# Where ScalarE puts the older rows' share of a token mix: the bank of the values, or an SBUF tile of its own

## The chip, the cores and the metric

The kernel runs on one NeuronCore of a Trainium2 chip. The metric is the device time of one execution in microseconds; lower is better. The engines are TensorE (PE, with its weight loads as PEld), VectorE (DVE), ScalarE (ACT), GpSimd (POOL) and SyncE (SP), which here only issues DMAs. Each engine works through its own queue in order and meets the others at semaphores.

## The reference

An attention with a soft cap is followed by a channel mix with a gate. Cut to what matters:

```python
def _attn_ref(q, k, v, cap):                    # (8, 12, 448, 64) each
    scores = cap * np.tanh(q @ k.T / sqrt(64) / cap)
    attn = np.exp(scores - scores.max(-1))
    attn = attn / (attn.sum(-1) + 1e-09)
    return attn @ v

def _moe_ref(x, mu_k, mu_r, w_k, w_v, w_r):     # x: (8, 448, 768)
    x_prev = concat([zeros, x[:, :-1]], axis=1)  # the row before
    xk = mu_k * x + (1.0 - mu_k) * x_prev
    xr = mu_r * x + (1.0 - mu_r) * x_prev
    k = np.maximum(xk @ w_k, 0.0)
    v = k * k @ w_v
    r = 1.0 / (1.0 + np.exp(-(xr @ w_r)))
    return r * v
```

The product `(1.0 - mu_k) * x_prev` in the line of `xk` is what the change is about.

## The kernel before

**Stages.** Up to about 510 us of the execution the kernel works through 48 pairs of heads (8 batches by 6 pairs; a pair fills 128 partitions, 64 channels of each of two heads, and its 448 tokens lie along the free dimension). In the same stretch it splits the weights into a high and a low part, and multiplies the mixed rows of the batch before by `w_k` (the matmuls on `kps`, K in the lists of steps). From about 510 us it finishes the last batch's product with `w_k` and then runs the products with `w_v` and `w_r` (line 702), which the change does not touch.

**A pair's way.** Scores of a pair's keys in groups of 128 (S0, S1, S2, and the last 64 keys of one or two pairs as S3) go into `s`, two PSUM tiles of two banks each. ScalarE applies tanh (line 290) and exp (line 303) into `p`. PE multiplies by the values into `pv` (V, lines 314 and 330). VectorE sums `p` with a transposing reduction (red, line 339); four small DMAs on SP gather these sums (line 345), VectorE ends them and inverts them (recip, lines 349 to 356), and they go out to DRAM (line 359) and come back spread over the partitions as `r` (line 368). Then three instructions follow each other on two engines:

```python
# norm, line 372, VectorE: reads pv (PSUM) and r, writes x
self.nc.vector.tensor_mul(self.X[i % 2][:, 1:], self.PV[i][:, 0:S], self.R.pop(i))
# mix_old, line 382, ScalarE: (1 - mu_k) * the row before, written over pv
self.nc.scalar.mul(self.xold, self.X[i % 2][:, 0:S], self.om["k"][:, hp:hp + 1])
# mix_new, line 387, VectorE: mu_k * x + xold
self.nc.vector.scalar_tensor_tensor(out=self.xk, in0=self.X[i % 2][:, 1:], scalar=self.mu["k"][:, hp:hp + 1],
                                    in1=self.xold, op0=ALU.mult, op1=ALU.add)
```

After mix_new GpSimd splits `xk` into `xkh` (line 124) and `xkl` (line 134), the operands of K. GpSimd also splits q and k of a later pair (`qkh` in line 124, `qkl` in line 134; `qkl` is a subtraction of two SBUF tiles over 896 columns) and the weights (`wkh`, `wkl`, line 584).

**What orders the work.** Each engine's queue is written out by hand as lists of step names (`STEP_0`, `STEP_6`, `STEP_7`, `ROWS`, `LAST` and others), one list per pair i; V in list i belongs to pair i-1, and norm, mix_old and mix_new to pair i-2. So in list i mix_old stands behind some tanh and exp on ScalarE, and mix_new behind some of the reductions and in front of the others, and of the weights' instructions, on VectorE.

**The bank.** `pv` has two buffers (`ps_v`, one bank each). V of pair k+2 therefore takes the bank that pair k had, and its first matmul waits for the last instruction that read or wrote that bank. In the kernel before that is mix_new of pair k, since `xold` lies in the bank. The pool `up` holds small SBUF tiles (`r`, `xk`, `xg`, `rs`), and `xk` has one buffer there.

Below, norm(k), mix_old(k) and mix_new(k) are those of pair k, and V(k) is its product with the values.

Of the kernel before, what the change touches and what calls it, by code (L numbers as in the profile page):

```python
# [10 lines left out]
F32 = mybir.dt.float32  # L11
# [6 lines left out]
B, H, S, D = 8, 12, 448, 64  # L18
# [11 lines left out]
P = 128  # L30
# [79 lines left out]
class Body:  # L110
# [263 lines left out]
    def mix_old(self, i):  # L374
        b, hp = i // NP, i % NP
        if hp == 0:
            xh = self.xkp[b % 2].tile([P, ND, S], F32R, name="xkh", tag="xkh")
            xl = self.xkp[b % 2].tile([P, ND, S], F32R, name="xkl", tag="xkl")
            self.XK[b] = (xh, xl)

        self.xold = self.PV.pop(i)[:, 0:S]
        self.nc.scalar.mul(self.xold, self.X[i % 2][:, 0:S], self.om["k"][:, hp:hp + 1])

    def mix_new(self, i):
# [682 lines left out]
```

## Time and profile before

| | |
|---|---|
| median of 3 runs | 908.24 us (905.85 to 908.97) |
| the profiled execution | 909.15 us, of which the span of the instructions is 907.3 us |
| PE busy | 873.5 us, 96% of the span |
| VectorE busy | 727.3 us, 80% |
| ScalarE busy | 624.0 us, 69% |
| GpSimd busy | 413.0 us, 46%, nearly all of it before 500 us |
| mean granted TensorE clock | 0.993 |

The profile is of one execution. "Busy" adds the instructions' durations; matmuls are pipelined, so a busy PE need not be at its peak. Idle time is put down to whatever the waiting instruction got last. A wait on an engine costs time only where the work that follows is itself on the way to the end, so the shares of this table say little on their own.

### The profile page before, as it was taken

Reading aid. Unit: us, or ns where it says so; the run is one execution under the profiler, and the core shown is the slowest. Engines: PE = TensorE matmul, PEld = TensorE weight load, DVE = VectorE, ACT = ScalarE, POOL = GpSimd, SP = SyncE. Lnnn points to the kernel's source line nnn. Section 1 sums busy time; section 2 is a strip of 40 time slices with the busy share of each in tenths; the row PEclk is TensorE's granted clock in tenths of the full one; section 3 lists DMA queues with packets and bytes.
Section 4 is the critical chain, followed back from the end, with each engine's and each line's share of the span. In section 5 each row is a group of like instructions: output and inputs, shape, how many; then the busy total and the mean of one; then the engine's idle time right before and its main releaser. Section 6 shows DMA issues by size and latency. Waiting matters only on the chain.

```text
span 907.3 us, 16778 instructions
## 1 busy us (share of the span) xinstructions
PE 873.5 (96%) x5826; PEld 703.6 (78%) x5826; DVE 727.3 (80%) x1246; ACT 624.0 (69%) x925; POOL 413.0 (46%) x345
## 2 busy tenths in 40 slices
PE   6889999999999999999999899999999999999996
PEld 2235666767767667667767699999999999999996
DVE  6888985988898998889878656787888667777775
ACT  8897887877878878788877365556565535555553
POOL 5895584777777776777763200000000024443330
PEclk9899999999999999999999999999999999999999
DMA  5465746676676767667566455745445546777663
GB/s 164 154 202 171 235 149 171 195 210 203 190 216 199 220 192 200 205 192 224 165 204 184 140 199 172 246 147 170 151 155 165 172 147 186 221 216 222 215 219 112
DMA packets 123679, 170.15 MB, mean 188 GB/s; under 512 B 22592, under 2 KB 107712, under 8 KB 123584
## 3 DMA queue, kind: packets, MB, share of 16 engines
q1 hardware_dynamic: 120992, 164.88, 59.6%
q10 hardware_dynamic: 2592, 4.10, 1.2%
q8 instruction: 48, 0.79, 0.4%
q14 instruction: 47, 0.39, 0.1%
HBM read 109.91 MB, written 56.60 MB: 184 GB/s over the span
## 4 chain that ended last, share of the span: by engine, by line
PE 58%; DVE 20%; DMA 8%; ACT 6%; SPq 4%; issue 4%; POOL 0%; DVEq 0%; ACTq 0%; POOLq 0%
PE ps L702 39%; DVE r L339 6%; PE kps L489 6%; PE pv L314 4%; DMA sq__195<-r 4%; PE kps L464 4%; SPq L345 3%; ACT p L303 3%; PE s L277 3%; ACT p L290 2%; DMA r<-rec_d 2%; DVE wsq L568 2%; DVE wa L571 2%; DMA rec_d<-rs 1%; DVE xk L387 1%
## 5 line engine op out<-in xcount | busy, mean ns | idle before, releaser
L290 ACT ACTIVATE p<-s,scl_t 128x896 f32<-128x896 f32 (+1 forms) x172 | 166.5, 980 | 37.0 <-PE s L277 20.9
L339 DVE TRANSPOSE_TENSOR_REDUCE r<-p 128x28 f32<-128x896 f32 (+1 forms) x192 | 180.1, 968 | 7.5 <-ACT p L303 7.0
L303 ACT ACTIVATE p<-p,cap_t 128x896 f32<-128x896 f32 (+1 forms) x172 | 174.4, 1023 | 4.3 <-ACT ko L501 0.4
L314 PE MATMUL pv<-p,rv 128*64 128x448 f32 x576 | 124.6, 562 | 14.3 <-DVE xk L387 14.2
L666 POOL TENSOR_TENSOR s<-src 128x384 f32<-128x384 f32 x14 | 14.3, 1020 | 266.3 <-DVE lo L687 266.3
L702 PE MATMUL ps<-wvh,hi 128*128 128x384 f32 x392 | 131.0, 334 | 0.0
L702 PE MATMUL ps<-wvl,hi 128*128 128x384 f32 x392 | 131.0, 334 | 0.0
L686 ACT CAST hi<-s 128x512 fp32r<-128x512 f32 (+1 forms) x112 | 63.6, 568 | 89.6 <-PE ps L702 76.9
L489 PE MATMUL kps<-xkh,wkh 64*128 64x448 f32 (+1 forms) x540 | 116.0, 370 | 3.3 <-ACT ko L501 3.3
L687 DVE TENSOR_TENSOR lo<-s,hi 128x512 fp32r<-128x512 f32 (+1 forms) x112 | 70.1, 626 | 59.4 <-ACT hi L686 43.8
L489 PE MATMUL kps<-xkh,wkl 64*128 64x448 f32 (+1 forms) x540 | 113.3, 362 | 0.0
L489 PE MATMUL kps<-xkl,wkh 64*128 64x448 f32 (+1 forms) x540 | 112.9, 361 | 0.0
L134 POOL TENSOR_TENSOR qkl<-rqk,qkh 128x896 fp32r<-128x896 f32 x47 | 100.4, 2136 | 10.2 <-ACT qkh L128 6.7
L702 PE MATMUL ps<-wrh,hi 128*128 128x384 f32 x294 | 98.9, 336 | 0.3 <-DVE o L725 0.3
L702 PE MATMUL ps<-wrl,hi 128*128 128x384 f32 x294 | 98.8, 336 | 0.0
L314 PEld LDWEIGHTS pv<-p,rv 128*64 128x64 f32 x576 | 36.5, 138 | 75.9 <-issue 48.6
L686 ACT CAST hi<-src 128x512 fp32r<-128x512 f32 (+1 forms) x84 | 47.8, 569 | 62.7 <-PE ps L702 59.7
L702 PE MATMUL ps<-wvh,lo 128*128 128x384 f32 x392 | 83.7, 334 | 0.0
L584 POOL TENSOR_TENSOR wsq<-wa,wsq 128x384 f32<-128x384 f32 (+1 forms) x40 | 54.3, 1357 | 54.6 <-DVE wsq L577 50.0
L489 PEld LDWEIGHTS kps<-xkh,wkh 64*128 64x128 f32 (+1 forms) x540 | 63.9, 184 | 18.0 <-ACT ko L501 6.4
L687 DVE TENSOR_TENSOR lo<-src,hi 128x512 fp32r<-128x512 f32 (+1 forms) x84 | 56.8, 677 | 21.5 <-ACT hi L686 19.3
L702 PEld LDWEIGHTS ps<-wvh,hi 128*128 128x128 f32 x392 | 73.6, 188 | 0.1
(118 smaller groups left out, 1928.0 us busy)
## 6 DMA issues: line engine op xcount, KB each, us to landing
rqk<-qk SPq DMA_DIRECT2D x47, 448.0 KB
src<-k_d SPq DMA_DIRECT2D x56, 256.0 KB
rv<-v SPq DMA_DIRECT2D x48, 256.0 KB
r<-rec_d SPq DMA_DIRECT2D x96, 112.0 KB
v_d<-o SPq DMA_DIRECT2D x56, 192.0 KB
src<-x_d SPq DMA_DIRECT2D x42, 256.0 KB
vl<-v_d SPq DMA_DIRECT2D x56, 192.0 KB
out<-o SPq DMA_DIRECT2D x55, 192.0 KB
```

Of the source, the lines that this page charges most:

```text
L134: {"p": self.nc.gpsimd, "v": self.nc.vector}[e].tensor_sub(*a)
L277: nc.tensor.matmul(s[:, (h + i) % 2, 0:S], qk[a][p, k], qk[b][p, 0:S], start=(n == 0), stop=(n == 2))
L290: self.nc.scalar.activation(p32[:, n], self.S.pop((i, g))[:, n, 0:S], AF.Tanh, scale=self.scl_t)
L303: self.nc.scalar.activation(p32, p32, AF.Exp, scale=1.0 if self.maxima else self.cap_t)
L314: nc.tensor.matmul(pv[p, 0:S], v[:, g, h, :], ph[:, (h + i) % 2, :], start=(g == 0), stop=False)
L339: self.nc.vector.tensor_reduce(out=r1[:, 0:RM].rearrange("p (x g) -> p x g", g=3)[:, :, g] if g < 3 else r1[:, RM:RC], in_=p32.rearrange(" ...
L464: nc.tensor.matmul(self.kps[fc][:, 0:S], w, m[:, dc, :], start=first, stop=last)
L489: self.nc.tensor.matmul(self.kps[c][:, 0:S], w[p, dc, c * P:(c + 1) * P], m[p, dc, :], start=s == 0, stop=last or way == 2 and t == 2, ski ...
L584: {"p": self.nc.gpsimd, "v": self.nc.vector}[e].tensor_add(sq, f(a), sq)
L686: self.nc.scalar.copy(hi, x)
L687: self.nc.vector.tensor_sub(lo, x, f(hi))
L702: self.nc.tensor.matmul(o, a[:, c, :], w[:, c, :], start=first and k == 0, stop=last and k == len(todo) - 1, skip_group_check=True)
```

## The change

ScalarE's product no longer overwrites the bank of the values. It goes into an SBUF tile `xold` of 128 by 448 floats with one buffer, from the pool `up`. The bank is no longer used after norm.

```diff
-        self.xold = self.PV.pop(i)[:, 0:S]
+        self.PV.pop(i)
+        self.xold = self.up.tile([P, S], F32, name="xold", bufs=1)
         self.nc.scalar.mul(self.xold, self.X[i % 2][:, 0:S], self.om["k"][:, hp:hp + 1])
```

So mix_old writes SBUF where it wrote PSUM; mix_new reads both of its inputs from SBUF where one came from PSUM; the first matmul of V(k+2) waits for norm(k) in place of mix_new(k); and mix_old(k+1) must wait until mix_new(k) has read the one buffer. No instruction is added, removed or reordered.

## Rows read from the trace of the kernel before

**Rows 1.** The page's head: span of all instructions.
```profile
span 907.3 us, 16778 instructions
```
**Rows 2.** Windows: stretch, busy time of each engine (instructions), granted clock, DMA share.
```profile
20.00:80.00 60.00, 49.85 (x260) 20.95 (x258) 52.89 (x89) 52.56 (x65) 51.03 (x45) 0.94 0.55 172
...
300.00:400.00 100.00, 97.70 (x810) 69.25 (x808) 89.33 (x156) 80.24 (x104) 73.94 (x58) 1.00 0.70 207
```
**Rows 3.** Waits: engine and line, releaser, total us, times, longest us.
```profile
POOL xkh L124 <- DVE xk L387: 83.5, 38, 8.6
...
PE pv L314 <- DVE xk L387: 14.2, 11, 3.4
```
**Rows 4.** Instructions by source line: count, duration in ns (min/median/max), first and last start.
```profile
L382 ACT ACTIVATE pv<-x,om_k x48: 618/639/644, 30.6 to 519.2; 128x448 f32<-128x448 f32 x48
...
L426 ACT ACTIVATE xl<-xo,om_r x14: 657/659/672, 548.0 to 713.8; 128x448 f32<-128x448 f32 x14
...
L387 DVE SCALAR_TENSOR_TENSOR xk<-x,mu_k,pv x48: 626/626/682, 32.0 to 519.9; 128x448 f32<-128x448 f32 x48
...
L399 DVE SCALAR_TENSOR_TENSOR xg<-x,mu_r,xg x34: 676/680/1341, 161.8 to 513.7; 128x448 f32<-128x448 f32 x34
```
**Rows 5.** The chain that ended last, first 560 us: start, us, what.
```profile
56.12 6.40 DMA rec_d<-rs
...
69.86 2.48 PE pv L314 x12
...
504.77 4.06 PE pv L314 x12
```
**Rows 6.** Timeline around 30 us: start, us, engine, line, tiles, [idle before <-releaser].
```profile
29.90 0.63 DVE L372 TENSOR_TENSOR x<-pv,r 128x448 f32<-128x448 f32 x1 [1.17 <-DMA r<-rec_d]
...
32.69 1.76 PE L314 MATMUL pv<-p,rv 128*64 128x448 f32 x4 [3.41 <-DVE xk L387]
```
**Rows 7.** Timeline of POOL and of DVE, 40 to 51 us.
```profile
40.33 2.12 POOL L134 TENSOR_TENSOR qkl<-rqk,qkh 128x896 fp32r<-128x896 f32 x1
...
49.55 2.10 POOL L134 TENSOR_TENSOR qkl<-rqk,qkh 128x896 fp32r<-128x896 f32 x1
...
40.92 0.64 DVE L387 SCALAR_TENSOR_TENSOR xk<-x,mu_k,pv 128x448 f32<-128x448 f32 x1
...
42.06 0.55 DVE L573 SCALAR_TENSOR_TENSOR wa<-w,kps 128x384 uint32<-128x384 uint32 x1
...
45.37 1.11 DVE L339 TRANSPOSE_TENSOR_REDUCE r<-p 128x28 f32<-128x896 f32 x1 [0.55 <-ACT p L303]
...
49.87 0.64 DVE L387 SCALAR_TENSOR_TENSOR xk<-x,mu_k,pv 128x448 f32<-128x448 f32 x1
```
**Rows 8.** Timeline of POOL, ACT and DVE, 67 to 92 us.
```profile
70.78 1.33 POOL L134 TENSOR_TENSOR xkl<-xk,xkh 128x448 fp32r<-128x448 f32 x1
...
89.54 2.13 POOL L134 TENSOR_TENSOR qkl<-rqk,qkh 128x896 fp32r<-128x896 f32 x1
...
86.43 1.16 ACT L501 ACTIVATE ko<-kps 128x448 f32<-128x448 f32 x2 [2.24 <-PE kps L464]
...
67.08 0.63 DVE L372 TENSOR_TENSOR x<-pv,r 128x448 f32<-128x448 f32 x1 [1.42 <-DMA r<-rec_d]
...
71.15 1.78 DVE L573 SCALAR_TENSOR_TENSOR wa<-w,wa 128x768 uint32<-128x768 uint32 x1
...
91.10 0.68 DVE L387 SCALAR_TENSOR_TENSOR xk<-x,mu_k,pv 128x448 f32<-128x448 f32 x1 [2.45 <-ACT pv L382]
```
**Rows 9.** Timeline around the last V, 498 to 514 us.
```profile
498.89 0.59 DVE L372 TENSOR_TENSOR x<-pv,r 128x448 f32<-128x448 f32 x1
...
503.92 1.04 ACT L303 ACTIVATE p<-p,cap_t 128x896 f32<-128x896 f32 x1
...
504.77 4.06 PE L314 MATMUL pv<-p,rv 128*64 128x448 f32 x12 [2.78 <-DVE xk L387]
...
513.67 0.54 ACT L501 ACTIVATE ko<-kps 128x448 f32<-128x448 f32 x1 [0.64 <-PE kps L464]
```

## The prediction, made before the result

> **What bounds the kernel now.** I began with the head of the page: the instructions span 907.3 us [rows 1], and the execution's own 909.15 us lies 1.85 us above that. Next the windows of the first stage, the only one that the change touches [rows 2]. From 20 to 80 us no engine is full: PE 49.85 of 60, VectorE 52.89, ScalarE 52.56, GpSimd 51.03. They hand work round in a ring. From 300 to 400 us PE has 97.70 of 100 and VectorE 89.33, so there PE is the bound and VectorE is not far behind it. The list of waits says what the bank costs: PE stood 14.2 us in 11 waits for mix_new before a V, while GpSimd stood 83.5 us in 38 waits for the same instruction and can afford it [rows 3]. Then the durations of the two instructions that change, with the nearest ones that already work in SBUF [rows 4].
>
> 14.2 us is not the gain. A wait counts only where it lies on the chain that ended last, and of the 11 only three are followed there by the V that they hold up: V(2), V(6) and V(47). V(6) and V(47) are shown [rows 5]. The other eight V are not in the chain: had they started sooner, PE would have stood later, for ScalarE or for GpSimd's weights.
>
> **What the earlier release is worth.** V(k+2) may start at the end of norm(k).
>
> V(2): norm(0) ends at 29.90 + 0.63 = 30.53, V(2) started at 32.69 after 3.41 us of standing [rows 6], so it can start 2.1 us sooner. ScalarE, fed by the scores behind V(2), would run about 1.2 us ahead at its next tanh. But VectorE is the slower one here: from 39 us on it works without a break but for 0.55 us at 45.37, where it waited for an exp [rows 7]. More than 0.55 us cannot be passed on.
>
> V(6): norm(4) ends at 67.08 + 0.63 = 67.71, V(6) started at 69.86 [rows 5, 8]: 2.1 us for PE. It is passed on, because ScalarE stands 2.24 us for PE's product at 86.43 and VectorE then 2.45 us for mix_old at 91.10 [rows 8]. 2.1 us.
>
> V(47): norm(45) ends at 499.48, PE has been free since 502.0, V(47) started at 504.77 and took 4.06 us [rows 9], where V(6) took 2.48 [rows 5]. After the change two of its three groups of keys can run from 502.0; the third needs the exp that ends at 503.92 + 1.04 = 504.96. A third of 2.48 us is 0.83, so V(47) would end at 505.8 and not at 508.83: 3.0 us. Next late is the bank of `kps` in the K that follows: its release, the relu at 513.67, came just after the product (0.64 us of standing) and stands on ScalarE behind mix_old(46), which ends at 513.03. A product that is ready 3 us sooner finds ScalarE still before mix_old(46), so the relu moves by 0.6 us only; PE, working 12 matmuls of 0.2 us on the other bank meanwhile, stands about 0.6 us. 2.4 us remain. After 510 us PE stands 0.3 us in all until about 900, so what arrives there arrives at the end.
>
> Gains: 2.1 + 2.4 = 4.5 us, and up to 0.55 at V(2).
>
> **What the SBUF tile costs.** mix_old: the like instruction that writes SBUF has a median of 659 ns, mix_old 639 [rows 4]: 20 ns by 48 is 1.0 us on ScalarE, which mostly hides behind its waits; 0.2 us on the chain. The wait for the one buffer costs nothing: mix_new(k) has ended a list earlier.
>
> mix_new alone: the nearest row with both inputs in SBUF is line 399, 680 ns against 626 [rows 4]; line 573 with one input in PSUM took 0.55 us for 384 columns [rows 7], which scaled to 448 is about mix_new's present length, so the lower end is nothing. Some 15 of the 48 mix_new lie in the chain: 0 to 0.8 us, I take 0.4.
>
> mix_new beside GpSimd is the large item. Line 573 with one input in PSUM starts at 42.06 while GpSimd is inside `qkl` (40.33 to 42.45), and takes its 0.55 us [rows 7]. With both inputs in SBUF it starts at 71.15 while GpSimd is inside `xkl` (70.78 to 72.11), and takes 1.78 us for twice the columns: it stands until GpSimd's instruction ends [rows 8]. Line 399 goes from 676 to 1341 ns at its worst [rows 4]. The mix_new of before runs beside GpSimd undisturbed, 682 ns at most; after the change it is of the second kind. The Trainium skill, "SBUF — State Buffer", section "Who interferes with whom", states this as a rule: a VectorE instruction with two SBUF inputs contends with a GpSimd instruction that reads SBUF, and the later one is held back. These rows agree.
>
> Over the timeline, 16 of 48 mix_new start inside a GpSimd instruction; what was left of it adds up to 9.1 us. In 38 GpSimd was itself waiting for `xk` [rows 3]; where both hold, `qkl` reached only 0.1 to 0.6 us into mix_new. The long ones lie early. mix_new(1) at 40.92 meets `qkl` until 42.45, 1.5 us; mix_new(2) at 49.87 meets one until 51.65, 1.8 us [rows 7]. VectorE is the slower engine there, so 1.5 less the 0.55 of slack is passed on, 0.95 us. For mix_new(2) and mix_new(3) it is a toss: GpSimd is late too, since it waits for `xk` and the weights from VectorE, and its `qkl` then starts within 0.2 us of mix_new's turn. First come, mix_new pays little; second, 1.9 us. Some of that is taken up by the trip of the reciprocals to DRAM, 6.40 us at 56.12 [rows 5], which other transfers hold up. I take 1.4 us for the three, with ends of 0 and 4.5.
>
> mix_new(6): ScalarE is 2.1 us sooner, but a GpSimd split in front of the `qkl` at 89.54 costs 0.4. Had mix_new come 0.6 us later, it would stand until that `qkl` ends at 91.67 [rows 8], and V(6)'s gain would be gone. mix_new(7), (8) and (9) meet a split of weights each, 0.3 us, 0.9 in all, in a stretch from 91 to 130 us in which VectorE never stands. mix_new(10) meets 1.66 us of `qkl`, which a wait for `r` behind it covers; uncovered, all of it would count. mix_new(11) meets 0.6 and holds up the reciprocals of the next pair: 0.5. Six later ones of 0.1 to 0.2 us: 0.3.
>
> Costs: 0.2 + 0.4 + 1.4 + 0.4 + 0.9 + 0.5 + 0.3 = 4.1 us.
>
> **Sum.** 909.15 - 4.5 + 4.1 = 908.75 us for an execution like the profiled one; the 0.55 of V(2) is already set against mix_new(1). The median of the runs is 0.91 us under that execution, so I forecast 907.8.
>
> **Rivals.** What a measurement here can tell from no change is 0.3%, 2.7 us.
>
> *The port is cheap, and the release is all.* If GpSimd's instruction only delays mix_new's start a little, or if mix_new comes first after the shift, the gains stand: 909.15 - 4.5 - 0.55 = 904.1, or 903.2 by the median; with 0.9 us for the lengths, 904.1. For it: most mix_new find GpSimd waiting. Against it: the 1.78 us of line 573.
>
> *VectorE held behind `qkl` becomes the bound of the first 70 us.* Place: mix_new(1), (2) and (3). Price: 1.5 + 1.9 + 1.9 less 0.55 is 4.75 us in place of 1.4; it decides if GpSimd's `qkl` starts first each time. That alone is 907.8 + 3.35 = 911.2, slower. For it: GpSimd works from 36 to 67 us without a break, and the two queues run in step. Against it: for mix_new(3) the order before was the other one. This is the rule of the skill just named, with each turn going against mix_new.
>
> *An input from SBUF is quicker.* If mix_new were 65 ns shorter, its share of the chain would give 15 by 65 ns = 1.0 us in place of costing 0.4, and the sum 906.4, still no change. The Trainium skill, "Perfetto Trace Analysis", section "Optimizing Scalar/DVE Operations", gives VectorE about 60 ns of access time on SBUF and 125 on PSUM, from which the 65 are estimated. Line 399, longer than mix_new [rows 4], speaks against it.
>
> *The bank is not released sooner.* If V(47) and V(6) waited for something beside mix_new, only costs would be left: 908.24 + 4.1 = 912.3. The release at the end of norm is plain in the order of the code, so it is the least likely.
>
> **How the numbers follow.** Gain and port about cancel (905.5 to 910.9, the likeliest's own range): 0.47, and the quicker input 0.02 within it. The release is all: 0.26. VectorE held behind `qkl`: 0.23. No earlier release: 0.04. So faster 0.26, same 0.47, slower 0.27. The range runs from 903.8, which keeps most of the first rival, whose full gains of 5.05 us and cheap lengths give 903.2 to 904.1, to 911.8, which takes in the second with a little of the lengths' upper end; about 1 in 10 is left on each side.
>
> **What would show it.** Right: no wait of PE for mix_new; V(47) starts by 502.1 and takes its last group at 505; V(6) starts within 0.1 us of norm(4)'s end; mix_new's median stays near 626 to 680 ns but its maximum goes to about 2 us, and the long ones are among mix_new(1) to (11), with `qkl` beside them; after V(47) PE stands for the relu for about 0.6 us. Wrong: mix_new's maximum below 0.8 us (the port term falls, and the time is near 904), or norm(4) more than 3 us later than before (the toss went against VectorE each time, and the time is over 911), or V(6)'s 2.1 us taken back before 130 us.

## The result, and the profile after

The change makes the kernel slower by half a per cent: 912.47 us median of 10 runs (909.69 to 916.73) against 907.9 us (10 runs of the kernel before), a ratio of 1.0052 with a 95% interval of 1.0033 to 1.0070. The forecast was 907.8 us, no change, with a range up to 911.8. The profiled execution took 915.32 us, 2.85 us above the median of its kernel, so its trace shows somewhat more loss than a typical execution. Lines of the changed kernel lie one higher from mix_old on: mix_old is line 383, mix_new 388, the relu 502, K 465 and 490.

The head of the page, beside [rows 1]:
```profile
span 913.5 us, 16777 instructions
```
The windows beside [rows 2]. From 20 to 80 us PE and VectorE are busy 2.4 and 1.8 us longer; from 300 to 400 us, where PE is the bound, PE is busy 0.9 us less, at a granted clock of 0.98 in place of 1.00:
```profile
20.00:80.00 60.00, 52.23 (x264) 21.28 (x260) 54.64 (x88) 52.45 (x65) 51.75 (x44) 0.94 0.53 172
300.00:400.00 100.00, 96.84 (x788) 67.90 (x784) 89.21 (x153) 78.73 (x102) 72.67 (x58) 0.98 0.69 201
```
The waits beside [rows 3]. PE's 14.2 us for mix_new are gone; 1.9 us for norm are left. PE's waits for the relu (before 3.3 us in 5, at most 0.7) are now fewer and longer:
```profile
POOL xkh L124 <- DVE xk L388: 84.7, 40, 8.6
...
PE kps L490 <- ACT ko L502: 6.1, 4, 2.7
...
PE s L277 <- ACT p L290: 5.7, 8, 2.1
...
PE pv L314 <- DVE x L372: 1.9, 2, 1.5
```
The durations beside [rows 4]. Alone, mix_new costs 10 ns more in the median with two SBUF inputs, mix_old 31 ns; only the maximum of mix_new is new:
```profile
L383 ACT ACTIVATE xold<-x,om_k x48: 652/670/674, 30.0 to 526.5; 128x448 f32<-128x448 f32 x48
...
L388 DVE SCALAR_TENSOR_TENSOR xk<-x,mu_k,xold x48: 629/636/2337, 31.5 to 527.2; 128x448 f32<-128x448 f32 x48
```
The timeline at mix_new(1), beside [rows 7]. It starts 0.25 us after `qkl` and ends 0.5 us behind the end of `qkl` at 42.24, so it stands nearly as long as `qkl` runs:
```profile
40.14 2.10 POOL L134 TENSOR_TENSOR qkl<-rqk,qkh 128x896 fp32r<-128x896 f32 x1
40.39 2.34 DVE L388 SCALAR_TENSOR_TENSOR xk<-x,mu_k,xold 128x448 f32<-128x448 f32 x1
```
The timeline at V(6), beside [rows 5, 8]. V(6) waits for nothing at 68.86, 1.4 us behind the end of norm(4) (0.1 us was predicted), but PE stood 2.14 us just before, for a tanh:
```profile
66.84 0.62 DVE L372 TENSOR_TENSOR x<-pv,r 128x448 f32<-128x448 f32 x1
...
68.05 0.47 PE L277 MATMUL s<-qkh 64*128 64x448 f32 x2 [2.14 <-ACT p L290]
68.86 1.47 PE L314 MATMUL pv<-p,rv 128*64 128x448 f32 x4
```
The timeline around 200 us, which the prediction did not look at. ScalarE stands 3.33 us for norm(16), then does mix_old and two exps, and only then the relu that PE needs; PE stands 2.68 us:
```profile
198.82 0.62 DVE L372 TENSOR_TENSOR x<-pv,r 128x448 f32<-128x448 f32 x1 [0.65 <-DMA r<-rec_d]
199.48 0.67 ACT L383 ACTIVATE xold<-x,om_k 128x448 f32<-128x448 f32 x1 [3.33 <-DVE x L372]
200.05 1.96 ACT L303 ACTIVATE p<-p,cap_t 128x896 f32<-128x896 f32 x2
201.92 0.95 ACT L502 ACTIVATE ko<-kps 128x448 f32<-128x448 f32 x2
...
202.49 1.17 PE L490 MATMUL kps<-xkh,wkh 64*128 64x448 f32 x2 [2.68 <-ACT ko L502]
```
The windows there: behind this stand TensorE is granted the lower of its two levels (1.2 GHz) for a while; (1 - 0.73) and (1 - 0.93) of 5 us are 1.7 us lost:
```profile
195.00:200.00 5.00, 4.81 (x48) 4.11 (x44) 3.79 (x5) 1.67 (x3) 4.28 (x3) 1.00 0.53 152
200.00:205.00 5.00, 2.51 (x13) 2.14 (x15) 4.03 (x9) 4.97 (x8) 2.08 (x4) 0.73 0.74 177
205.00:210.00 5.00, 5.00 (x35) 2.91 (x33) 4.86 (x9) 2.38 (x4) 3.81 (x4) 0.93 0.59 191
```
The timeline of V(47), beside [rows 9]. It runs as predicted, two groups at once and the third at the end of the exp. Behind it PE stands 0.48 us for the relu (0.6 predicted) and then 1.03 us for a later one (not predicted):
```profile
509.26 1.72 PE L314 MATMUL pv<-p,rv 128*64 128x448 f32 x8
...
512.34 0.97 PE L314 MATMUL pv<-p,rv 128*64 128x448 f32 x4 [1.36 <-ACT p L303]
...
521.02 0.47 PE L465 MATMUL kps<-xkh,wkh 128*128 128x448 f32 x1 [0.48 <-ACT ko L502]
...
534.89 0.47 PE L465 MATMUL kps<-xkh,wkh 128*128 128x448 f32 x1 [1.03 <-ACT ko L502]
```

### The profile page after: what moved, and what is told of

Read it like the earlier page. It is cut to its first block, busy times and chain, and to the rows that moved or that the text cites. A ratio compares the mean times of both kernels' runs of the same rounds, so it can differ in the third digit from the quotient of the medians.

```text
span 913.5 us, 16777 instructions
## 1 busy us (share of the span) xinstructions
PE 879.0 (96%) x5826; PEld 705.9 (77%) x5826; DVE 734.3 (80%) x1246; ACT 624.9 (68%) x925; POOL 414.0 (45%) x345
## 4 chain that ended last, share of the span: by engine, by line
PE 60%; DVE 15%; DMA 9%; ACT 6%; SPq 4%; issue 3%; POOL 2%; DVEq 0%; ACTq 0%; POOLq 0%
PE ps L703 39%; PE kps L490 8%; DVE r L339 5%; PE pv L314 5%; DMA sq__195<-r 4%; PE s L277 3%; PE kps L465 3%; SPq L345 2%; ACT p L303 2%; ACT p L290 2%; DMA r<-rec_d 2%; DMA rqk<-qk 1%; DVE xk L388 1%; DMA rec_d<-rs 1%; DVE sq__195 L349 1%
## 5 line engine op out<-in xcount | busy, mean ns | idle before, releaser
L490 PE MATMUL kps<-xkh,wkh 64*128 64x448 f32 (+1 forms) x540 | 118.4, 375 | 7.5 <-ACT ko L502 6.1
L490 PE MATMUL kps<-xkh,wkl 64*128 64x448 f32 (+1 forms) x540 | 115.4, 366 | 0.0
L490 PE MATMUL kps<-xkl,wkh 64*128 64x448 f32 (+1 forms) x540 | 114.9, 366 | 0.0
```

The lines of the kernel that those rows point to most:

```text
L490: self.nc.tensor.matmul(self.kps[c][:, 0:S], w[p, dc, c * P:(c + 1) * P], m[p, dc, :], start=s == 0, stop=last or way == 2 and t == 2, ski ...
```

## The experiments

My theory after the result: in the first 145 us mix_new stands behind GpSimd and VectorE and PE fall behind; V(47) is a gain; and some 5 us between pairs 12 and 47 come from the earlier release, which lets PE reach the next stand sooner. The rivals: those 5 us belong to the one execution that was profiled, or they too come from the two SBUF inputs. The place of `xold` is chosen in Python for each pair, so the change can be made for some pairs only. Ratios are to the kernel before, timed beside it, with 95% intervals.

**The change by stretches of pairs.** In these three runs line 382 is undone for the other pairs:
```diff
-        self.PV.pop(i)
-        self.xold = self.up.tile([P, S], F32, name="xold", bufs=1)
+        pv = self.PV.pop(i)
+        self.xold = self.up.tile([P, S], F32, name="xold", bufs=1) if i == 45 else pv[:, 0:S]
```


> Only pair 45 writes its older rows' share to SBUF; the other 47 keep the bank of the values. My theory is that the last release is a plain gain and that the loss lies in the pairs ahead of it. Then V(47) starts about 2.7 us sooner, the stage ends 2.85 us sooner as in the changed kernel, less up to 1.03 us for the new stand of TensorE for line 502's `ko`: 1.8 to 2.8 us faster than the kernel before, a ratio of 0.997 to 0.998. Rival, that what is gained at V(47) is given back before the product with w_k ends: a ratio within 0.001 of 1.

Measured: 906.69 us, 0.9987 (0.9971 to 1.0003). It is 0.8 us below the median of the kernel beside it, less than half of the least that was expected, and the interval does not tell it from nothing.

With the condition `i < 12`:

> Only pairs 0 to 11 write to SBUF. If mix_new standing behind GpSimd is a real cost there, and V(6)'s 2.1 us are swallowed by it, the shift against the kernel before is about 2.4 us at pair 11, as in the changed kernel, and stays to the end: slower by 2 to 3 us, a ratio of 1.002 to 1.003. Rival, that the early shift of the changed kernel belonged to the one execution that was profiled: mix_new(1) still stands about 1.5 us, but the shift is gone by pair 11 and the ratio is within 0.001 of 1. If V(6) counts and mix_new(1) does not, 2 us faster.

Measured: 910.14 us, 1.0022 (1.0004 to 1.0039), as expected. In its trace PE is 2.5 us behind the kernel before at 145 us (the table below).

With the condition `12 <= i < 45`:

> Only pairs 12 to 44 write to SBUF. In the profile of the changed kernel some 4.8 us were lost between pairs 12 and 47 in two places, where TensorE stood once for long (2.68 and 1.70 us) for line 502's `ko` and the matmuls behind it ran 1.3 us slower. If the change makes these, this kernel is slower by 4 to 5 us, a ratio of 1.004 to 1.0055. Rival, that they belong to that one execution (its clock was 0.988 against 0.993): a ratio within 0.001 of 1, and no shift between pairs 12 and 47.

Measured: 911.02 us, 1.0038 (1.0017 to 1.0060). The middle is no accident of one execution, though the one profiled here (906.95 us) lost almost nothing: the times of this kernel reach from 906.95 to 916.50 us. The mean granted clock is lower than in the kernel before: 0.9898 in 12 runs against 0.9929 in 35.

**The inputs without the release.** All pairs in SBUF; the bank held behind mix_new:
```diff
-        self.PV.pop(i)
...
                                             in1=self.xold, op0=ALU.mult, op1=ALU.add)
+        t = self.up.tile([1, 1], F32, name="held", bufs=1)
+        self.nc.vector.tensor_copy(t, self.PV.pop(i)[0:1, 0:1])
```


> All pairs write to SBUF, but a VectorE copy of one element out of the bank behind mix_new keeps the bank until then, as before; the price is 48 short instructions, some 15 of them on the path, about 1 us in all. So this has the two SBUF inputs without the earlier release. If the early loss is GpSimd holding mix_new, it is 4.5 us at pair 11 (the 2.4 seen, and V(6)'s 2.1 which no longer stand against it); if the middle loss is the release, there is no further shift from pair 12 to 47; V(47) gains nothing. That gives 5 to 6 us slower, a ratio of 1.0055 to 1.0065. Rival, that the earlier release makes the loss and the SBUF inputs cost nothing: about 1 us slower, a ratio of 1.001.

Measured: 911.41 us, 1.0047 (1.0030 to 1.0063). Less than expected, and it does not decide alone, since the copies may not be free (line 390 of this kernel by source: minimum, median, maximum):
```profile
L390 DVE COPY held<-pv x48: 137/140/142, 32.2 to 525.0; 1x1 f32<-1x1 f32 x48
```
The start of the same matmul against the kernel before, in us, read from the traces (matmul 720 is at 145 us, 3480 at 487 us and 4500 at 670 us there):
```
matmul            360    720   3480   4500
after           +0.70  +2.05  +5.78  +6.64
pairs 0-11      -1.69  +2.47  +2.87  +3.18
all, held       +0.40  +2.25  +4.19  +3.80
pairs 12-44     -2.32  -1.90  -2.48  -1.70
pair 45 only    -1.35  -0.93  +0.22  -0.62
```
The last two have the early stage of the kernel before, and are 1 to 2 us ahead of it by 145 us. By 145 us the three with early pairs in SBUF are at 2.26 in the mean, and the kernel before and the last two at -0.94: an early loss of 3.2 us, not the 2.4 read from the first pair of traces. A microsecond of one trace is scatter, and PE's start there is not yet the time at the end.

**The relu out of the way.** If the middle is lost at PE's stands for `ko`, the relu sooner should give it back:
```diff
-... 3:relu 01345:mix_old mix_new x_high x_low gate_old
-exp2 red2 weight_rest weight_sum 024:exp3 024:red3 0:relu weight_abs ...
+... 3:relu 01345:mix_old 0:relu mix_new x_high x_low gate_old
+exp2 red2 weight_rest weight_sum 024:exp3 024:red3 weight_abs ...
```
On the changed kernel:

> The change as it is (all pairs in SBUF), and in the five lists i = 18, 24, 30, 36 and 42 the relu moves from behind two exps to right behind mix_old on ScalarE. My theory of the middle is that the V that no longer waits for mix_new only lets TensorE reach the next stand sooner, for `ko`, where it then stands once for 1.5 to 2.7 us; there the granted clock may fall, 1.7 us for each fall. With the relu two exps sooner the stands of line 490 for `ko` fall below 0.5 us, no window from 160 to 500 us has a clock below 0.97, and the time is 4 to 5 us under the changed kernel, near 908: a ratio of 1.000 to 1.001 to the kernel before. Rival, that the middle is held by something that the relu does not order (the trip of the reciprocals): TensorE stands as long at another line and the ratio stays at 1.005.

Measured: 911.85 us, 1.0048 (1.0026 to 1.0070). The rival came true. Waits of PE from 150 to 500 us:
```profile
PE kps L490 <- ACT turned L497: 2.4, 2, 1.8
PE kps L490 <- POOL xkl L134: 1.8, 4, 0.6
```
The stands for `ko` are gone and no window of 5 us between 160 and 500 us has a clock below 0.97, as expected; but PE now stands for the split of `xk` and at line 497, and the time is the same.

On the kernel before:

> The kernel before, with only the relu of those five lists moved. It stood there five times for 0.5 to 0.7 us, 3.3 us in all, with no fall of the clock; the stands at V for mix_new remain. 2 to 3 us faster, a ratio of 0.997 to 0.998. Rival, that these stands are not on the way to the end: a ratio within 0.001 of 1.

Measured: 904.38 us, 0.9972 (0.9955 to 0.9989), as expected: with the bank kept, the same edit is worth 2.8 us. PE's waits from 150 to 500 us are then for mix_new:
```profile
PE pv L314 <- DVE xk L387: 7.9, 8, 1.6
PE kps L464 <- ACT ko L501: 0.3, 1, 0.3
```
With the relu moved and `xold` in SBUF for `i >= 12`:

> Pairs 0 to 11 keep the bank, pairs 12 to 47 write to SBUF, and the relu is moved. If the three parts add up (early 2.6 us not paid, the middle freed of its stands for mix_new and for `ko`, V(47) sooner) this is the fastest of all: 903 to 905 us, a ratio of 0.995 to 0.997. If the SBUF inputs in the middle cost by themselves (GpSimd beside mix_new), about as the kernel before with the relu moved, or slower.

Measured: 907.91 us, 1.0005 (0.9983 to 1.0027). The parts do not add up: it is 3.5 us above the kernel with the relu moved and the bank kept, so taking PE's waits for mix_new away brought nothing here either.

**The early pairs.** Pairs 0 to 11 in SBUF, and `qkl` in two halves:
```diff
-        self.sub(e, lo, self.raw[i], f(hi))
+        for c in (slice(0, S), slice(S, S + KC)) if i < 14 else (slice(0, S + KC),):
+            self.sub(e, lo[:, c], self.raw[i][:, c], f(hi)[:, c])
```


> Pairs 0 to 11 write to SBUF as in the run on the early pairs alone (910.1 us), and GpSimd makes `qkl` of pairs 1 to 13 in two instructions of 448 columns in place of one of 896. If what costs is that mix_new stands until GpSimd's instruction in flight ends, its longest falls from 2.3 to about 1.3 us, and of the 2.6 us about half is left: a ratio of 1.001. GpSimd pays for 13 more instructions, some 0.1 us each by its two `xkl` and `qkl` durations (2 by 1.15 against 2.12). Rival, that the stands themselves do not matter (the loss is the clock falling behind the stand at 132 us): still 1.002 or more.

Measured: 909.46 us, 1.0026 (1.0010 to 1.0042). mix_new by source, first with halves (line 389), then whole (line 388 of the run on pairs 0 to 11):
```profile
L389 DVE SCALAR_TENSOR_TENSOR xk<-x,mu_k,xold x12: 645/849/1569, 31.4 to 146.6; 128x448 f32<-128x448 f32 x12
```
```profile
L388 DVE SCALAR_TENSOR_TENSOR xk<-x,mu_k,xold x12: 643/869/2278, 31.2 to 147.8; 128x448 f32<-128x448 f32 x12
```
The longest stand shrinks by 0.7 us, the median hardly, and the time stays within the intervals. Which mix_new stands longest differs from execution to execution: (0) in the first of these two, (5) in the second, (1) in the changed kernel. That the one long stand is not what costs is suggested by this, and not shown: 0.7 us is less than the intervals can tell.

With the condition `i < 6`, and `6 <= i < 12`:

> Only pairs 0 to 5 write to SBUF. By the starts of the same matmul in ten profiled executions, the kernels with early pairs in SBUF are only about 0.9 us behind the others at 85 us (scatter 1 us), though mix_new(1) stands 1.5 us there: V(2) and V(6) pay part of it. 0 to 1 us slower, a ratio of 1.000 to 1.001. Rival, that the whole early loss is mix_new(1): 1.003.

Measured: 908.09 us, 1.0010 (0.9992 to 1.0028).

> Only pairs 6 to 11 write to SBUF. Between 85 and 145 us the kernels with these pairs in SBUF lost 1.4 to 4.2 us, the others 0 to 0.5: mix_new stands 0.2 to 0.4 us behind a split of weights each time, VectorE has no slack there, GpSimd's next weights come later by the sum, and TensorE stands 1.1 us in place of 0.2 at 132 us, behind which the clock may fall. 2 to 3 us slower, a ratio of 1.002 to 1.0035. Rival, that it is made by pairs 0 to 5: 1.000.

Measured: 908.95 us, 1.0021 (1.0002 to 1.0041). By the medians most of the early loss is made by pairs 6 to 11, but the two intervals overlap. The traces say the same: from 85 to 145 us the six kernels with pairs 6 to 11 in SBUF lost 1.3 to 4.2 us against the kernel before, the one with pairs 0 to 5 alone 1.1 us, and the twelve others at most 0.4. All six mix_new stand a little (by source; 626 ns in the kernel before):
```profile
L388 DVE SCALAR_TENSOR_TENSOR xk<-x,mu_k,xold x6: 816/874/1078, 91.1 to 146.6; 128x448 f32<-128x448 f32 x6
```
The timeline of pairs 6 to 11 in SBUF shows one place where PE then stands longer:
```profile
131.88 0.51 POOL L124 TENSOR_SCALAR wkh<-wsq 128x384 fp32r<-128x384 f32 x1
132.44 0.47 PE L465 MATMUL kps<-xkh,wkh 128*128 128x448 f32 x1 [1.08 <-POOL wkh L124]
...
133.55 0.47 PE L465 MATMUL kps<-xkh,wkl 128*128 128x448 f32 x1 [0.63 <-POOL wkl L134]
```
In the kernel before the first of the two stands was 0.16 us and the second 0.64. Behind the first the granted clock fell in two profiles, those of pairs 0 to 11 with `qkl` whole and in halves, and cost 1.7 us more; in the profile shown and in the changed kernel it did not fall there.

**What V(6) and V(47) are worth.** The bank kept but for pair 45, and for pairs 4 and 45, with the relu moved:

> The relu of the five lists moved (904.4 us alone), and pair 45 alone in SBUF (0.8 us faster alone). If the two are independent: 903.6 us, a ratio of 0.996. Rival, that what V(47) brings is taken back in the stretch behind it (the stands for `ko` of 0.4 to 1.0 us at about 514 and 528 us come later by less than V(47) comes sooner): no faster than with the relu alone, 0.997.

Measured: 904.15 us, 0.9971 (0.9955 to 0.9987): the rival came true. In its timeline V(47) ends early, and PE gives 1.6 us of it back at two later stands, which the kernel with the relu alone does not have:
```profile
499.75 0.97 PE L314 MATMUL pv<-p,rv 128*64 128x448 f32 x4 [1.36 <-ACT p L303]
508.53 0.47 PE L465 MATMUL kps<-xkh,wkh 128*128 128x448 f32 x1 [0.62 <-ACT ko L502]
522.37 0.48 PE L465 MATMUL kps<-xkh,wkh 128*128 128x448 f32 x1 [1.01 <-ACT ko L502]
```


> As the kernel beside it, with pair 4 in SBUF too, so V(6) starts at the end of norm(4). My prediction passed V(6)'s 2.1 us on to the end: 2 us faster than the kernel beside it. Rival, which the profile of the changed kernel suggests, where TensorE stood 2.14 us for an exp just before that V: V(6) is then held by its own scores and values, and the time is that of the kernel beside it within 0.1%.

Measured: 903.22 us, 0.9952 (0.9935 to 0.9969). By the medians it is 0.9 us below the kernel beside it, at the edge of the rival's 0.1%, and within the intervals. It has the best median of all that were run, but it can't be told from the kernel with the relu alone.

**The middle, inputs and release apart.** Three kernels with one copy of one element behind mix_new of pairs 12 to 44: control (bank, copy from the bank), inputs (SBUF, copy from the bank), inputs and release (SBUF, copy from `self.X[i % 2]`). The diff is that of the inputs.
```diff
-        self.PV.pop(i)
-        self.xold = self.up.tile([P, S], F32, name="xold", bufs=1)
+        self.xold = self.up.tile([P, S], F32, name="xold", bufs=1) if 12 <= i < 45 else self.PV[i][:, 0:S]
...
                                             in1=self.xold, op0=ALU.mult, op1=ALU.add)
+        pv = self.PV.pop(i)
+        if 12 <= i < 45:
+            t = self.up.tile([1, 1], F32, name="held", bufs=1)
+            self.nc.vector.tensor_copy(t, pv[0:1, 0:1])
```


> The kernel before, with a VectorE copy of one element out of the bank behind mix_new of pairs 12 to 44: the control of the two above. 33 copies of 0.14 us (4.46 us for 32 in the run with all pairs held) on VectorE, which is not the bound there: 0 to 1 us slower, a ratio of 1.000 to 1.001.

> Pairs 12 to 44 write to SBUF, and a VectorE copy of one element out of the bank behind mix_new holds the bank until then: two SBUF inputs in the middle without the release. Its like with the copy and no other change is the run with the bank and a copy. If the release is what costs in the middle (3.5 us in the run on the middle pairs), it stands within 0.1% of that one; if the SBUF inputs cost, 3 us or more above it.

> The same with the one-element copy taken from `x` in SBUF, so the bank is released behind norm: inputs in SBUF and the release. If the release costs, 2 to 4 us above the held one, with a mean granted clock that is 0.002 to 0.003 lower, and the stands for `ko` at 1.2 to 2.7 us in place of 0.7; and a stand of 1.2 to 2.2 us for line 497 near 495 us, which all four kernels with the middle released had and none of the others. Rival, that the earlier 3.5 us were scatter between chip jobs: the three kernels with a copy within 0.1% of each other.

Measured: control 906.09 us, 0.9984 (0.9967 to 1.0001); inputs 907.07 us, 1.0004 (0.9982 to 1.0026); inputs and release 910.34 us, 1.0045 (1.0027 to 1.0063). The release costs 3.3 us by the medians, and the intervals of the last two do not overlap. The inputs cost 1 us by the medians and 1.8 by the ratios, which these intervals do not tell from nothing. The timelines show the stands run together; the first two lines are with the bank held, the last is released:
```profile
186.75 2.48 PE L314 MATMUL pv<-p,rv 128*64 128x448 f32 x12 [0.96 <-DVE held L392]
...
197.19 0.90 PE L493 MATMUL kps<-xkh,wkh 64*128 64x448 f32 x2 [0.57 <-ACT ko L505]
```
```profile
197.89 0.90 PE L493 MATMUL kps<-xkh,wkh 64*128 64x448 f32 x2 [2.06 <-ACT ko L505]
```
Of the expectation's signs two failed. The mean granted clock was no lower (0.9919 in 10 runs against 0.9923 in 12), and the stand for the copy that is line 497 in the changed kernel was 0.92 us. Another was seen: the reciprocals of pair 40 were stored at the same time in both, and their load could be issued 1.46 us later with the release (SyncE's timelines, held and released):
```profile
437.93 0.34 SPq L359 DMA_DIRECT2D rec_d<-rs  x1
439.74 1.84 SPq L368 DMA_DIRECT2D r<-rec_d  x2
```
```profile
437.94 0.34 SPq L359 DMA_DIRECT2D rec_d<-rs  x1
441.20 1.12 SPq L368 DMA_DIRECT2D r<-rec_d  x2
```
This delay cost nothing there, since norm(40) started at the same time in both (VectorE's timelines, held and released):
```profile
445.39 0.59 DVE L372 TENSOR_TENSOR x<-pv,r 128x448 f32<-128x448 f32 x1
```
```profile
445.40 0.58 DVE L372 TENSOR_TENSOR x<-pv,r 128x448 f32<-128x448 f32 x1
```
With the conditions `36 <= i < 45`, `12 <= i < 45` (another profile of the same kernel) and `12 <= i < 36`:

> Only pairs 36 to 44 write to SBUF. In the four profiles with the middle released the reciprocals of pairs 40, 42 and 43 took 2 to 3.7 us from their store to the issue of their load, where the six others have 1.3 to 1.8, norm(44) came 1.3 to 2.6 us later against TensorE, and TensorE stood 1.2 to 2.0 us for line 497 near 495 us. If the release of these pairs does it, both are here too and it is 1 to 2 us slower, 1.001 to 1.002. Rival, that it is set by the pairs from 12 on: no stand there, 1.000.

Measured: 908.82 us, 1.0019 (1.0003 to 1.0035). Slower as expected and the trip of pair 40 (from the issue of its reciprocals' store to that of their load) is 2.7 us, but without the stand at line 497. PE stands 1.93 us for `ko` at 451.25 in its place, and the clock is 0.77 and 0.89 in the two windows of 5 us behind.

> Pairs 12 to 44 in SBUF once more, for another profiled execution: the first profile of this kernel was of its fastest execution (906.95 us, median 911.0), and so was that of the middle released with a copy (907.84, median 910.3). If the loss is the clock falling behind a stand for `ko`, this one has one or two windows between 160 and 500 us with a clock below 0.97, each 1.7 us. If it is the trips of the reciprocals, it has none, and the loss lies at pairs whose trip is longer than in the kernel before.

Measured: one execution, 909.82 us. It is the first case: the clock falls twice, behind stands of 1.73 us at 198.40 and 1.88 us at 325.55. The windows:
```profile
195.00:200.00 5.00, 3.27 (x31) 2.48 (x29) 3.79 (x9) 4.61 (x7) 2.92 (x3) 1.00 0.58 159
200.00:205.00 5.00, 5.00 (x29) 3.40 (x27) 4.86 (x10) 3.26 (x5) 3.89 (x4) 0.66 0.62 207
320.00:325.00 5.00, 3.67 (x38) 3.05 (x34) 2.86 (x6) 2.52 (x5) 3.11 (x3) 1.00 0.73 181
325.00:330.00 5.00, 4.45 (x25) 4.01 (x27) 4.83 (x11) 4.93 (x8) 3.34 (x3) 0.66 0.73 219
```


> Pairs 12 to 35 write to SBUF, pairs 36 to 44 do not. All of 12 to 44 cost 3.5 us, 36 to 44 alone 1.3 us. If the loss adds up over the pairs: 2 us slower, a ratio of 1.002 to 1.0025, and the trip of pair 40 is 1.8 us again. If it is all in the late third: a ratio within 0.001 of 1.

Measured: 908.43 us, 1.0015 (0.9991 to 1.0039), between the two cases. The median is that of the kernel beside it (908.50), the ratio would be 1.4 us, and neither case is told from the other: that the loss is spread over the pairs is not shown. The trip of pair 40 is 1.8 us, as expected. PE waited for `ko` alone, 8.6 us in 5 waits, at most 2.62; behind one of 1.93 us at 389.64 the clock was 0.66 for 5 us. The twelve times part in two: seven from 905.42 to 908.60 us, five from 911.52 to 913.11 us, and those five have clocks of 0.988 to 0.993, the seven of 0.991 to 0.995.

## Why the prediction was wrong

- **The step that failed.** "The other eight V are not in the chain: had they started sooner, PE would have stood later". That was right as a mechanism, and priced at nothing. What the runs showed in its place: in the middle the release costs 3.3 us (inputs and release against inputs), and 3.5 us by the run on pairs 12 to 44. Two short stands, at a V and some 10 us later for the relu, become one (0.96 and 0.57 us against 2.06). Nothing is won by the earlier V. My reading, argued and not shown, is that PE is held there by a ring of reciprocals, norm, mix and split that V's start does not shorten: ScalarE stood 3.33 us for norm(16) ahead of the relu at 200 us, and without the relu's stand PE stood for the split of `xk` instead. Where the single stand is long, the clock may fall, 1.7 us each time. That is seen between 160 and 495 us six times in four of the eight profiles with a middle released, behind stands of 1.70 to 2.68 us, and in none of the twelve with the bank kept or held there, whose stands reach 1.62 us. Five other stands of 1.72 to 2.62 us in the same eight profiles were followed by no fall.
- **What stays open.** How the 3.3 us come about. Six falls in eight executions are 1.3 us each, not 3.3. The mean clocks disagree: in the run on pairs 12 to 44, 0.0031 less is, as an estimate, 2.8 of its 3.5 us, but the released kernel with a copy had hardly a lower clock than the held one. The kernels with the relu moved lost time with no fall in the profile; theirs shows a stand at line 497 near 499 us (1.81 and 1.97 us). All three profiled executions with just pairs 12 to 44 released (906.95, 907.84 and 909.82 us) are faster than the medians of these kernels (911.02 and 910.34), so no trace shows their typical loss. The longer trip of pair 40 is in all seven profiles with pairs 36 to 44 released (2.2 to 3.7 us), and it is 1.8 us in the thirteen others. It carries little: norm(40) starts 7.5 to 7.6 us behind the store in five of the seven, as with the bank kept, and waits for `r` only in the two with the relu moved, where the longer wait is this:
```profile
448.68 0.63 DVE L372 TENSOR_TENSOR x<-pv,r 128x448 f32<-128x448 f32 x1 [1.25 <-DMA r<-rec_d]
```
- **V(47), "2.4 us remain".** The start, the third group's exp and the stand of 0.6 us came as predicted; the worth by the medians is 0.2 to 0.8 us, neither told from nothing (0.9987 alone; 904.15 against 904.38 with the relu moved). Two things were missed. The 4.06 us of V(47) were 2.48 and a fall of the clock (0.66 from 505 to 510 us): in the run on pairs 0 to 11 the same V took 2.48 us behind a stand of 2.77 us (its timeline):
```profile
507.95 2.48 PE L314 MATMUL pv<-p,rv 128*64 128x448 f32 x12 [2.77 <-DVE xk L388]
```
There only 2.77 + 2.48 - (1.72 + 1.36 + 0.97) = 1.2 us are to be won. And the sum "PE stands 0.3 us in all until about 900" was read with V(47) late: once V(47) ends sooner, PE stands 1.0 us for the relu of the next bank. That stand is in all six profiles in which V(47) is released sooner, and also in the five in which it starts late but runs in 2.48 us.
- **V(6), 2.1 us.** In the profile after, PE stood 2.14 us for a tanh just ahead of V(6). The 2.23 us of standing were also long by luck: in twelve other profiles with pairs 0 to 5 in the bank PE stood 0 to 2.22 us there, 1.15 in the median. Its worth with all else kept was 0.9 us, not told from nothing.
- **The port, 4.1 us with its lengths.** With V(2) and V(6) bringing little, the early pairs cost 3.2 us by 145 us in the traces and 2.6 us in the medians, so the size was about right. The place was half right: mix_new(1) stood as described, mix_new(2) and (3) came first (0.65 and 0.64 us), and the small stands of mix_new(6) to (11), priced at 1.8 us, carry most of it by the medians (1.5 us against 0.7), with GpSimd's weights late behind them. The Trainium skill, "SBUF — State Buffer", section "Who interferes with whom", says that a VectorE instruction with two SBUF inputs contends with a GpSimd instruction that reads SBUF, and that the order of issue decides which one is held. The 2.34 us of mix_new(1), which came second, and the 0.65 us of mix_new(2), which came first, agree. Behind 150 us the longest mix_new of the run on pairs 12 to 44 is 0.69 us: there GpSimd waits for `xk` and does not collide.
- **The lengths, 0.2 and 0.4 us.** 31 ns for mix_old and 10 ns for mix_new, 0.6 us over 15 pairs: as priced.
- **The rivals.** The time came out on the side of "VectorE held behind `qkl`", but not by its mechanism: it put the loss in mix_new(1) to (3), and pairs 0 to 5 cost 0.7 us, not told from nothing. "The port is cheap" fell with the early runs, and "an input from SBUF is quicker" with the 636 ns.

The sum from the runs: by the medians 2.6 (early) + 3.5 (middle) - 0.8 (V(47)) = 5.3 us, beside 4.6 measured; by the ratios 2.0 + 3.4 - 1.2 = 4.2, beside 4.7.

## What to carry to other kernels

A wait that does not lie on the chain is not free to remove: ask which wait the engine meets next, and whether two short stands become one long one, since the clock may fall behind it. A gain read from one stand in one profile should be looked for in other executions of the same stage; here the V(6) that carried it stood longer than in twelve others, and the V(47) was long by the clock. And before a buffer is released sooner, look for the instruction in a queue that the bound engine waits for: moving the relu two exps ahead brought 2.8 us, the release none.

## What was not expected of the hardware

- A stand of the same length was followed by a fall of the granted clock in some executions and not in others. In the fourteen profiles in which V(47) waits for its bank until mix_new it does so for 2.77 to 2.86 us; in nine of them the clock falls and V(47) takes 3.88 to 4.17 us, in five it does not and V(47) takes 2.48 us. Each fall in the middle cost 1.7 us of matmuls.
- A VectorE copy of a single element takes 140 ns; yet 33 of them in the middle did not slow the kernel (0.9984).
- The maximum of mix_new beside a halved `qkl` was 1.57 us, and beside a whole one 2.28: both ended 0.5 us behind the end of the `qkl` that was in flight.
